# FFN squares, normalised rows and softmax products moved from VectorE to GpSimd in a two-layer attention + FFN kernel

One core of one Trainium2 chip. The metric is the device time of one execution in microseconds (us); lower is better. Every timed run quoted here is of the fast state except where it is said; a program on one core that was run once has no known state.

## What the kernel computes

Two identical layers over x of shape 1 x 2048 x 448 in bf16, each of them attention with 16 heads of 28 and an FFN of 1792:

```python
x = x + A(layernorm(x), wqkv, wo)            # softmax(q k^T * 28**-0.5) v, then wo
x = x + B(layernorm(x), w1, b1, w2, b2)      # relu(x w1 + b1)**2 w2 + b2
# ... the same two lines again
```

Of the kernel before, what the change touches and what calls it, by code (L numbers as in the profile page):

```python
# [13 lines left out]
ALU = mybir.AluOpType  # L14
# [187 lines left out]
def kernel(  # L202
# [12 lines left out]
    nc = tc.nc  # L215
    _, S, D = A_x.shape
# [39 lines left out]
    x_sb = const.tile([P, NTB, D], DT.bfloat16, name="x_sb")  # L256
# [163 lines left out]
    def layernorm(t0, nt, deps_of, early=False, mv=None):  # L420


        if mv is None:
            mv = moments()
            for j in range(nt):
                yield stats(mv, t0, j, deps_of(j))
        ln = {}
        single = early and t0 == 0 and TILES
        rss = []
        for a, b in [(0, 1), (1, 2)] if single else [(0, nt)]:  # L430
            def rsqrt(e, a=a, b=b):
                rstd = sp.tile([P, 4], DT.float32, name="rstd")
                for j in range(a, b):
                    ln[j] = rstd[:, j:j + 1]
                ve = sp.tile([P, 4], DT.float32, name="ve")
                nc.gpsimd.tensor_tensor(out=ve[:, a:b], in0=mv[0][:, a:b, 1], in1=eps_t[:, a:b], op=ALU.add)  # L436
                nc.gpsimd.tensor_tensor(out=rstd[:, a:b], in0=ve[:, a:b], in1=mhalf[:, a:b], op=ALU.pow)  # L437
            rs = Op("POOL", 0.95 if early else 0.6, rsqrt, deps=[mv[1][b - 1]], sets=[("rs", t0 + a)] if early else ())
            rss += [rs] * (b - a)
            pl.spawn(EV, iter([rs]))  # L440
        box = {}

        def take(e):
            box["x"] = xtp.tile([P, NDC, QR], DT.bfloat16, name="xnT")
        own_xt = Op("DVE", 0.0, take, acq=R_xt)
        yield own_xt
        xnT = box["x"]
        ends = []
        todo = []
        evs = []  # L450

        def turn(p0, own, xs):
            box = {}

            def tr(e, xs=xs):
                tp = bank(t, "tp").bitcast(DT.bfloat16).rearrange("p (c q) -> p c q", c=NDC)
                box["t"] = tp
                for k, (xn, _) in enumerate(xs):
                    for dc in range(NDC):
                        nc.tensor.transpose(out=tp[:, dc, k * P:(k + 1) * P],  # L460
                                            in_=xn[:, dc * P:(dc + 1) * P], identity=ident[:, :])
            t = Op("PE", 0.07 * NDC * len(xs), tr, deps=[x[1] for x in xs],
                   acq=pools_now(early) if early else spare(1))
            yield t

            def ev(e, p0=p0, w=len(xs) * P):
                tp = box["t"]
                dst = xnT[:, :, p0 * P:p0 * P + w]
                if e == "ACT":
                    nc.scalar.copy(out=dst, in_=tp[:, :, 0:w])  # L470
                else:
                    nc.vector.tensor_copy(out=dst, in_=tp[:, :, 0:w])
            o = Op("DVE", 0.12 + 0.3 * len(xs), ev, deps=[t], rel=t, sets=[("xT", t0 + p0)] if early else ())
            ends.append(o)
            evs.extend([o, Op("DVE", 0.0, None, deps=[t], rel=own)])

        wide = 1 if single else 2
        for p0 in range(0, nt, wide):
            js = range(p0, min(p0 + wide, nt))
            own = Op("DVE", 0.0, None, acq=R_xn)  # L480
            yield own
            xs = []
            for j in js:
                xn = xns[2 * (own.turn % 2) + j % 2]

                def norm(e, j=j, xn=xn):
                    nc.vector.tensor_scalar(out=xn[:, 0:D], in0=x_sb[:, t0 + j, :],  # L487
                                            scalar1=mv[0][:, j, 0:1], scalar2=ln[j],
                                            op0=ALU.subtract, op1=ALU.mult)
                nm = Op("DVE", 0.42, norm, deps=[rss[j]], sets=[("n", t0, j)] if early else ())  # L490
                yield nm
                xs.append((xn, nm))

            todo.append((p0, own, xs))
            if early and p0 + wide < nt:
                continue
            while todo:
                p0, own, xs = todo.pop(0)
                yield from turn(p0, own, xs)
        yield from evs  # L500
        return xnT, own_xt, ends
# [140 lines left out]
    for pi, (l, qb, g, kbs, first, last) in enumerate(passes):  # L642
        r = 4 // blocks[l][qb][1]
# [182 lines left out]
    oTn_of = {}  # L826
# [81 lines left out]
    def norm_stream(l, qb, g, res, oe):  # L908


        t0, nt = blocks[l][qb]
        n = nt * P
        box = {}
        tail = qb == len(blocks[l]) - 1
        if (l, qb) not in oTn_of:
            def take(e):
                oTn_of[l, qb][0] = np_.tile([P, G, QR], DT.bfloat16, name="oTn")
            oTn_of[l, qb] = [None, Op("DVE", 0.0, take, acq=R_on)]
            yield oTn_of[l, qb][1]
        if tail:  # L920
            def den(e):
                box["t"] = bank(d, "den")
                nc.tensor.matmul(box["t"][:, 0:n], lhsT=sel[:, :], rhs=res["t"][:, 0:n], start=True, stop=True)
            d = Op("PE", 0.1 + n * 4 / 2400, den, deps=[oe], acq=pools_now())
            yield d

            def rcp(e):
                box["r"] = rp.tile([P, QR], DT.float32, name="rec")
                nc.vector.reciprocal(out=box["r"][:, 0:n], in_=box["t"][:, 0:n])  # L929
            r = Op("DVE", n * 0.0066, rcp, deps=[d], rel=d, acq=R_rec)  # L930
            own = r
            yield r
        else:
            w = n // DHP

            def spread(e):
                box["d"] = sp.tile([P, QR // DHP], DT.float32, name="dn")
                nc.sync.dma_start(out=box["d"][:, 0:w],
                                  in_=res["t"][DH::DHP, 0:n])
            d1 = Op("DMA", 0.5, spread, deps=[oe], lat=0.5)  # L940
            yield d1

            def rcp(e):
                nc.vector.reciprocal(out=box["d"][:, 0:w], in_=box["d"][:, 0:w])
            r1 = Op("DVE", 0.25, rcp, deps=[d1])
            yield r1

            def away(e):
                box["s"] = dp.tile([P, w], DT.float32, name=f"scr{w}")
                nc.sync.dma_start(out=box["s"][:, :], in_=box["d"][:, 0:w])  # L950
            d2 = Op("DMA", 0.4, away, deps=[r1], lat=-0.5)
            yield d2

            def back(e):
                box["r"] = rp.tile([P, QR], DT.float32, name="rec")
                src = box["s"][:, :].rearrange("(h a) j -> h (a j)", h=G)
                nc.sync.dma_start(out=box["r"][:, 0:n], in_=src.unsqueeze(1).to_broadcast([G, DHP, n]))
            r = own = Op("DMA", 0.5, back, deps=[d2], acq=R_rec, lat=2.7)
            yield r
        def mul(e):  # L960
            nc.vector.tensor_tensor(out=oTn_of[l, qb][0][:, g, 0:n], in0=res["t"][:, 0:n],  # L961
                                    in1=box["r"][:, 0:n], op=ALU.mult)
        m = Op("DVE", 0.1 + n / 960, mul, deps=[r, oTn_of[l, qb][1]], rel=oe)
        yield m
        yield Op("DVE", 0.0, None, deps=[m], rel=own)
        norm_done.setdefault((l, qb), []).append(m)
        if len(norm_done[l, qb]) == G:
            pl.spawn(LASTP if (l, qb) == (1, len(blocks[1]) - 1) else NLP + 0.1 * (qb - len(blocks[1])) if l == 1 and qb >= len(blocks[1]) - NL else 4 + 0.1 * qb, chain(l, qb))
# [6 lines left out]
    def chain(l, qb):  # L975


        t0, nt = blocks[l][qb]
        n = nt * P
# [20 lines left out]
        for f0 in range(0, NFC, pack):  # L1000
            fcs = range(f0, min(f0 + pack, NFC))
            w = len(fcs) * n
            b = {}
# [7 lines left out]
            def square(e, b=b, w=w, f0=f0):  # L1011
                r = b["r"]
                b["h"] = h = hidden(f0 // pack)
                nc.vector.tensor_tensor(out=h[:, 0:w], in0=r[:, 0:w], in1=r[:, 0:w], op=ALU.mult)

            def then(o, b=b, square=square):
                b["s"] = Op("DVE", 0.42, square, deps=[o], rel=o)
                return b["s"]
            o = yield from mm_tile(
                [(i * n, n, [(w1[:, dc, fc * P:(fc + 1) * P], xnT[:, dc, 0:n]) for dc in range(NDC)])  # L1020
                 for i, fc in enumerate(fcs)],
                relu, 0.70, [*ends, ("w1",)], True, post=[then], acq=R_r)
# [86 lines left out]
```

## The kernel before

All of x, K, Q, V and the weights live in SBUF. The softmax takes no maximum; the row sums come out of the product with V through a column of ones. The order of the instructions on every engine is fixed when the program is built: a planner (a greedy list scheduler) simulates the engines with durations written in the code, and emits instructions in the order in which its simulation starts them. `Op("DVE", 0.42, fn)` means: on VectorE, planned at 0.42 us, emitted by `fn`. Each engine is given its own queue in that order, and semaphores make it wait for what it needs, so a wrong duration does not make a wrong result; it makes an engine stand before something that the plan took for ready.

The parts that matter (cut):

```python
def e_stream():        # ScalarE: exp of three score tiles (128 x 512 each) at a time
    nc.scalar.activation(out=pt[:, 0:n], in_=gbuf[gi]["sc"][:, 0:n], func=AF.Exp, ...)

def a_first / a_rest:  # an "aside": exp of a fourth tile by VectorE, seven instructions
    tensor_scalar(vi<-PSUM); tensor_scalar(vm<-vi); tensor_scalar(vi<-vi)
    3 x scalar_tensor_tensor(vh <- (vh + b) * vm); scalar_tensor_tensor(p <- (vh + b0) * vi)
# an aside is planned only while VectorE's planned load over 12 us is under BUSY=0.95 (or BB=0.85)

def layernorm(...):    # two row tiles j of a block
    norm: nc.vector.tensor_scalar(out=xn[:, 0:D], in0=x_sb[:, t0 + j, :], scalar1=mean, scalar2=rstd,
                                  op0=ALU.subtract, op1=ALU.mult)        # Op("DVE", 0.42)
    tr:   8 x nc.tensor.transpose(out=tp[...], in_=xn[...], identity=ident)  # PE, waits for both norms
    ev:   nc.vector.tensor_copy(out=xnT, in_=tp)                         # then q, k, v or the FFN

def mul(e):            # 1/rowsum, per head group
    nc.vector.tensor_tensor(out=oTn, in0=oT_sb, in1=rec, op=ALU.mult)    # Op("DVE", 0.1 + n / 960)

def square(e):         # FFN
    nc.vector.tensor_tensor(out=h[:, 0:w], in0=r[:, 0:w], in1=r[:, 0:w], op=ALU.mult)  # Op("DVE", 0.42)

def heat():            # extra matmuls on an xn tile, put where the plan has PE idle
```

The softmax here doesn't subtract the row's maximum and nothing guards it: scores larger than these inputs give would overflow.

## Time and profile before

| | before |
|---|---|
| time, median of 2 (range) | 924.38 us (923.94 to 924.81) |
| span of the profiled execution | 921.5 us |
| exponentials on ScalarE | 659 instructions, 886.2 us |
| ScalarE idle just before them | 5.5 us |
| first exponential starts / last one ends before the end of the span | 11.2 us / 17.0 us |
| asides on VectorE | 73 |
| mean granted clock of PE | 1.000 |

How to read it: the last rows make a sum. Head (11.2) + exponentials (886.2) + idle before them (5.5) + tail (17.0) + 1.6 of other ScalarE work between is the span. The same sum for the changed kernel says where its time goes. The tail is found in ScalarE's timeline: twelve exponentials start at 888.94 and last 15.56 us, so the last ends at 904.50. In a line of the waits, the numbers are us in total, times, and the longest:

```profile
ACT pt L755 <- PE sc L737: 3.2, 6, 0.9
```

### The profile page before, as it was taken

How to read it: one execution, taken by the hardware profiler on the slowest of the kernel's cores; microseconds unless marked ns; L12 is line 12 of the kernel's file. 1: busy time of each engine (PE TensorE's matmuls, PEld its weight loads, DVE VectorE, ACT ScalarE, POOL GpSimd, SP SyncE). 2: the span in 40 equal slices, each digit the busy share in tenths (PEclk: the TensorE clock that was granted, in tenths of full speed). 3: DMA queues.
4: the chain of work that ended last, by engine and by line, in shares of the span. 5: the costliest groups of instructions: out<-in, count | busy, mean ns of one | idle time of the engine just before them, and what ended most of it. 6: DMA issues, size and time to landing. Idle time of an engine off the chain costs nothing.

```text
span 921.5 us, 32836 instructions
## 1 busy us (share of the span) xinstructions
PE 860.8 (93%) x14796; PEld 515.4 (56%) x14796; DVE 672.2 (73%) x1387; ACT 896.2 (97%) x678; POOL 39.7 (4%) x89
## 2 busy tenths in 40 slices
PE   8999989999999999899999999989999999999998
PEld 4555656555555555555546455556465465546566
DVE  7754678788877887777857564577887788888355
ACT  6999999999999999999999999999999999999994
POOL 5100000000000000000000000000000000000000
DMA  7200010000000000000000000011000000000100
GB/s 228 64 2 2 3 43 17 15 10 12 15 14 8 14 13 10 14 12 5 2 2 2 2 2 2 6 36 38 16 18 18 28 10 24 14 20 13 25 14 17
DMA packets 33000, 18.67 MB, mean 20 GB/s; under 512 B 17498, under 2 KB 32411, under 8 KB 32860
## 3 DMA queue, kind: packets, MB, share of 16 engines
q1 hardware_dynamic: 32860, 16.58, 6.3%
q8 instruction: 115, 1.88, 0.8%
q14 instruction: 25, 0.20, 0.1%
HBM read 14.26 MB, written 2.07 MB: 18 GB/s over the span
## 4 chain that ended last, share of the span: by engine, by line
ACT 66%; PE 17%; issue 12%; DVE 2%; DMA 2%; POOL 0%; SPq 0%; ACTq 0%; DVEq 0%
ACT pt L755 66%; PE sc L737 6%; PE mt L521 5%; PE oT L878 3%; DMA dn<-oT_sb 2%; PE sc L521 1%; PE tp L460 1%; DVE xn L487 0%; DMA x_sb<-in_A_x_dram 0%; DVE st L414 0%; PE mt L737 0%; DVE oTn L961 0%; PE mt L1060 0%; DVE x_sb L972 0%; POOL rstd L437 0%
## 5 line engine op out<-in xcount | busy, mean ns | idle before, releaser
L755 ACT ACTIVATE pt<-sc 128x1536 bf16<-128x1536 f32 x659 | 886.2, 1508 | 5.5 <-PE sc L737 3.2
L737 PE MATMUL sc<-Q_sb,K_sb 32*128 32x256 bf16 (+1 forms) x7576 | 384.0, 266 | 51.8 <-ACT pt L755 48.7
L737 PEld LDWEIGHTS <-K_sb 32*128 32x128 bf16 x7882 | 214.9, 92 | 218.0 <-issue 209.1
L878 PE MATMUL oT<-pt,V_sb 128*32 128x256 bf16 (+1 forms) x4204 | 149.6, 268 | 0.7 <-DVE rec L929 0.3
L878 PEld LDWEIGHTS <-V_sb 128*32 128x32 bf16 x4352 | 92.5, 96 | 43.6 <-issue 40.9
L521 PE MATMUL mt<-xnT,w 128*128 128x256 bf16 (+1 forms) x896 | 115.7, 270 | 0.6 <-DVE r L1010 0.3
L807 DVE SCALAR_TENSOR_TENSOR vh<-vh,vm 128x512 f32<-128x512 f32 x146 | 99.9, 684 | 1.7
L521 PEld LDWEIGHTS <-w 128*128 128x128 bf16 x952 | 79.4, 98 | 32.0 <-issue 23.3
L1010 DVE TENSOR_SCALAR r<-mt 128x512 bf16<-128x512 f32 x106 | 72.5, 684 | 29.8 <-PE mt L521 29.2
L784 DVE TENSOR_SCALAR vi<-mt 128x512 int32<-128x512 f32 x73 | 50.2, 687 | 31.4 <-PE mt L737 30.0
L972 DVE TENSOR_TENSOR x_sb<-x_sb,mt 128x448 bf16<-128x448 bf16 (+1 forms) x63 | 38.4, 609 | 32.1 <-PE mt L521 31.3
L521 PE MATMUL mt<-w,h 128*128 128x448 bf16 x224 | 52.8, 355 | 0.0
L521 PE MATMUL mt<-w,V_sb 128*128 128x448 bf16 (+1 forms) x224 | 50.8, 351 | 0.0
L807 DVE SCALAR_TENSOR_TENSOR vh<-vm 128x512 f32<-128x512 f32 x73 | 49.6, 680 | 0.0
L737 PE MATMUL mt<-Q_sb,K_sb 32*128 32x256 bf16 (+1 forms) x306 | 48.8, 269 | 0.0
L436 POOL TENSOR_TENSOR ve<-mv,eps_t 128x2 f32<-128x2 f32 (+1 forms) x34 | 8.0, 235 | 867.6 <-DVE mv L415 867.6
L900 DVE COPY oT_sb<-oT 128x256 f32<-128x256 f32 (+1 forms) x48 | 19.2, 400 | 33.2 <-PE oT L878 32.8
L414 DVE BATCH_NORM_STATS2 st<-x_sb 128x6 f32<-128x448 bf16 x64 | 39.3, 615 | 1.3 <-DMA x_sb<-in_A_x_dram 0.8
L543 DVE CAST K_sb<-mt 128x512 bf16<-128x512 f32 (+1 forms) x30 | 20.4, 680 | 21.4 <-PE mt L521 21.3
L487 DVE TENSOR_SCALAR xn<-x_sb,mv,rstd 128x448 bf16<-128x448 bf16 x64 | 25.9, 420 | 10.9 <-POOL rstd L437 8.3
L521 PE MATMUL mt<-xnT,wq 128*128 128x256 bf16 x248 | 33.5, 274 | 0.0
L521 PE MATMUL mt<-xnT,wk 128*128 128x256 bf16 x240 | 32.6, 274 | 0.5 <-DVE K_sb L900 0.4
(89 smaller groups left out, 649.7 us busy)
## 6 DMA issues: line engine op xcount, KB each, us to landing
rec<-scr SPq DMA_DIRECT2D x56, 128.0 KB
x_sb<-in_A_x_dram SPq DMA_DIRECT2D x8, 224.0 KB
out_dram<-x_sb SPq DMA_DIRECT2D x15, 112.0 KB
w<-in_B_w_dram SPq DMA_DIRECT2D x1, 1568.0 KB
w<-in_B_w_dram SPq DMA_DIRECT2D x1, 1344.0 KB
dn<-oT_sb SPq DMA_DIRECT2D x56, 4.0 KB
scr<-dn SPq DMA_DIRECT2D x56, 4.0 KB
V_sb<-in_A_wqkv_dram SPq DMA_DIRECT2D x1, 672.0 KB
```

The lines of the kernel that those rows point to most:

```text
L414: nc.vector.bn_stats(out=st[:, :], in_=x_sb[:, t0 + j, :])
L487: nc.vector.tensor_scalar(out=xn[:, 0:D], in0=x_sb[:, t0 + j, :], scalar1=mv[0][:, j, 0:1], scalar2=ln[j], op0=ALU.subtract, op1=ALU.mult)
L521: nc.tensor.matmul(box["t"][:, c0:c0 + n], lhsT=lhsT() if callable(lhsT) else lhsT, rhs=rhs, start=a, stop=b)
L543: nc.vector.tensor_copy(out=dst, in_=src)
L737: nc.tensor.matmul(dst[k][:, i * nt * P:(i + 1) * nt * P], lhsT=K_sb[l][rows, g, (kb + i) * P:(kb + i + 1) * P], rhs=Q_sb[rows, g, t0 * P: ...
L755: nc.scalar.activation(out=pt[:, 0:n], in_=gbuf[gi]["sc"][:, 0:n], func=AF.Exp, scale=float(np.log(2.0)) * 2.0 ** -23)
L784: nc.vector.tensor_scalar(out=box["i"][:, :], in0=src, scalar1=EXP_BIAS, scalar2=0.0, op0=ALU.add, op1=ALU.max)
L807: nc.vector.scalar_tensor_tensor(out=h[:, :], in0=src, scalar=b, in1=m, op0=ALU.add, op1=ALU.mult)
L878: nc.tensor.matmul(box["t"][DHP * hh:DHP * hh + DHP, 0:n], lhsT=V_sb[l][:, kb + i, 4 * g + hh, :], rhs=p[:, c0:c0 + n], start=begin and kb ...
L900: nc.vector.tensor_copy(out=dst, in_=src)
L972: nc.vector.tensor_tensor(out=x_sb[:, tb, lo:hi], in0=x_sb[:, tb, lo:hi], in1=t[:, 0:hi - lo], op=ALU.add)
L1010: nc.vector.tensor_scalar(out=r[:, 0:w], in0=t[:, 0:w], scalar1=0.0, scalar2=None, op0=ALU.max)
```

## The change

Intent: VectorE carries evacuations from PSUM and the asides; GpSimd is 96% idle. Take elementwise work that touches SBUF alone to GpSimd, and let the planner fill the freed VectorE time with asides. The planner is told what GpSimd is thought to take.

```diff
 def norm(e, j=j, xn=xn):
-    nc.vector.tensor_scalar(out=xn[:, 0:D], in0=x_sb[:, t0 + j, :],
+    (nc.vector if early else nc.gpsimd).tensor_scalar(out=xn[:, 0:D], in0=x_sb[:, t0 + j, :],
                             scalar1=mv[0][:, j, 0:1], scalar2=ln[j],
                             op0=ALU.subtract, op1=ALU.mult)
-nm = Op("DVE", 0.42, norm, ...)
+nm = Op("DVE" if early else "POOL", 0.42 if early else 0.7, norm, ...)
 ...
 def mul(e):
-    nc.vector.tensor_tensor(out=oTn_of[l, qb][0][:, g, 0:n], ...)
+    (nc.vector if tail else nc.gpsimd).tensor_tensor(out=oTn_of[l, qb][0][:, g, 0:n], ...)
-m = Op("DVE", 0.1 + n / 960, mul, ...)
+m = Op("DVE" if tail else "POOL", 0.1 + n / (960 if tail else 400), mul, ...)
 ...
-    nc.vector.tensor_tensor(out=h[:, 0:w], in0=r[:, 0:w], in1=r[:, 0:w], op=ALU.mult)
+    nc.gpsimd.tensor_tensor(out=h[:, 0:w], in0=r[:, 0:w], in1=r[:, 0:w], op=ALU.mult)
-    b["s"] = Op("DVE", 0.42, square, deps=[o], rel=o)
+    b["s"] = Op("POOL", 1.2, square, deps=[o], rel=o)
```

More of the change, by code (lines that the diff above doesn't have):

```diff
@@ L486, in norm @@
                 def norm(e, j=j, xn=xn):
-                    nc.vector.tensor_scalar(out=xn[:, 0:D], in0=x_sb[:, t0 + j, :],
+                    (nc.vector if early else nc.gpsimd).tensor_scalar(out=xn[:, 0:D], in0=x_sb[:, t0 + j, :],
                                             scalar1=mv[0][:, j, 0:1], scalar2=ln[j],
                                             op0=ALU.subtract, op1=ALU.mult)
-                nm = Op("DVE", 0.42, norm, deps=[rss[j]], sets=[("n", t0, j)] if early else ())
+                nm = Op("DVE" if early else "POOL", 0.42 if early else 0.7, norm, deps=[rss[j]], sets=[("n", t0, j)] if early else ())
                 yield nm
@@ L960, in mul @@
         def mul(e):
-            nc.vector.tensor_tensor(out=oTn_of[l, qb][0][:, g, 0:n], in0=res["t"][:, 0:n],
+            (nc.vector if tail else nc.gpsimd).tensor_tensor(out=oTn_of[l, qb][0][:, g, 0:n], in0=res["t"][:, 0:n],
                                     in1=box["r"][:, 0:n], op=ALU.mult)
-        m = Op("DVE", 0.1 + n / 960, mul, deps=[r, oTn_of[l, qb][1]], rel=oe)
+        m = Op("DVE" if tail else "POOL", 0.1 + n / (960 if tail else 400), mul, deps=[r, oTn_of[l, qb][1]], rel=oe)
         yield m
```

## The prediction

> **What bounds the kernel now.** I read the page first: busy shares, the chain that ended last, the groups.
>
> ```profile
> PE 860.8 (93%) x14796; PEld 515.4 (56%) x14796; DVE 672.2 (73%) x1387; ACT 896.2 (97%) x678; POOL 39.7 (4%) x89
> ...
> ACT 66%; PE 17%; issue 12%; DVE 2%; DMA 2%; POOL 0%; SPq 0%; ACTq 0%; DVEq 0%
> ...
> L755 ACT ACTIVATE pt<-sc 128x1536 bf16<-128x1536 f32 x659 | 886.2, 1508 | 5.5 <-PE sc L737 3.2
> L784 DVE TENSOR_SCALAR vi<-mt 128x512 int32<-128x512 f32 x73 | 50.2, 687 | 31.4 <-PE mt L737 30.0
> ```
>
> ScalarE does one exponential after another: 659 instructions fill 886 of 921 us and wait 5.5 us in all. So the time is a head (about 10 us before the exponentials start), the exponentials, and a tail. VectorE is not the bound: nothing that only empties it shows directly. But it takes work from ScalarE. The 73 `vi` instructions are units of scores (128x512) whose exponential VectorE computes, seven instructions each; I call one an aside. An exponential instruction holds three units, so an aside saves ScalarE 886.2/659/3 = 0.449 us.
>
> The schedule is made when the program is built, by a list scheduler with durations written in the code. It admits an aside only when VectorE's planned load over the last 12 us is under 0.95 (0.85 in two stretches), when a PSUM bank is free, and when a buffer for the result is free. That decides what freed VectorE time is worth, so next I asked for busy time by stretches of 40 us, and for the waits of PE.
>
> ```profile
> core 0: us, PE busy (x) PEld busy (x) DVE busy (x) ACT busy (x) POOL busy (x), PEclk, DMA share, GB/s
> ...
> 200.00:240.00 40.00, 38.04 (x612) 21.95 (x600) 33.18 (x69) 40.00 (x31) 1.77 (x4) 1.00 0.05 13
> ...
> 560.00:600.00 40.00, 38.64 (x647) 22.56 (x647) 19.83 (x41) 39.54 (x31) 1.06 (x4) 1.00 0.02 6
> ```
>
> ```profile
> PE sc L737 <- ACT pt L755: 48.7, 129, 0.9
> PE tp L460 <- DVE xn L487: 1.3, 2, 1.1
> ```
>
> There are two kinds of stretch. From 120 to 440 us and from 640 to 840 us VectorE is 80 to 82% busy and 58 of the 73 asides start (the same view restricted to `vi`: 22+12+24); there its load limits them. From 440 to 600 us it falls to 50% with few asides: other gates bind, and freed time buys nothing. PE hardly waits for VectorE, and its whole reserve against ScalarE is 48.7 us.
>
> [...]
>
> ```profile
> L487 DVE TENSOR_SCALAR xn<-x_sb,mv,rstd x64: 365/391/1740, 5.4 to 910.8; 128x448 bf16<-128x448 bf16 x64
> ```
>
> ```profile
> 305.50 0.55 POOL L436 TENSOR_TENSOR ve<-mv,eps_t 128x2 f32<-128x2 f32 x1 [43.26 <-DVE mv L415]
> ```
>
> ```profile
> 305.34 0.66 DVE L807 SCALAR_TENSOR_TENSOR vh<-vm 128x512 f32<-128x512 f32 x1
> ```
>
> The 1740 ns normalisation (median 391; the columns are min/median/max) is one of a run begun at 13.42 us, beside GpSimd's 1.60 us memset of 14.26 us. The 0.55 us GpSimd add (0.20 elsewhere) began inside a two-input VectorE instruction and ended when it did. [...]
>
> **Part by part.** Removed from VectorE: 111 squares of 512 at 0.417 and two of 256 at 0.283 = 46.9 us; 60 normalisations (64 less four marked early) at the median 0.391 = 23.5; 56 products at 0.414 and four narrow ones at 0.280 = 24.3 (the last block of each layer keeps its products). Together 94.7 us in 233 instructions. Neighbours overlap on VectorE by about 0.08 us (starts of 0.42 us instructions are 0.34 apart in the timeline), so the real gain is 94.7 - 233 x 0.08 = 76 us.
>
> Added to GpSimd, [...] product 0.75; normalisation 0.7. Sum 113 x 1.3 + 60 x 0.7 + 60 x 0.75 = 234 us, with the 40 of before 30% of the span. GpSimd is no bound. The diff plans 1.2, 0.7 and 0.74, nearly the same, so the plan is honest about GpSimd [...].
>
> Gain: the same view restricted to the squares puts 36 + 30 = 66 of 113 (58%) in the dense stretches; I take the same share for the rest, so 0.58 x 94.7 = 55 us are freed there. An aside costs 0.687+0.421+0.424+0.680+3 x 0.684 = 4.26 us; 55/4.26 = 13 more if every microsecond were used. Banks and result buffers remain, so I choose 60%: 8 more, 81 in all, minus 8 x 0.449 = **3.6 us**.
>
> [...] One aside spans about 4.8 us (170.53 to 175.33 in the timeline), so 58 x 4.8 = 278 of 520 dense us, 53%. There 66 squares and 68 other moved instructions start, 134; 134 x 0.53 = 71 fall into an aside. If each costs VectorE 0.7 us [...], that is 50 us, against 0.58 x 76 = 44 freed. So VectorE is not really freer, and with 8 more asides is fuller than the plan says. [...] I guess that a quarter of the 50 us reaches PE (12 us) and half of that is taken by PE's reserve: **plus 6 us** of ScalarE idle. This is the softest number.
>
> Cost in the tail, where nothing hides: at the end the last block's FFN has squares at 913.94, 914.83 and 915.88 (two), the last done about 916.5. At 1.3, 1.3, 1.3 and 0.75 us in one queue from 914.0 they end near 918.6; the final products run meanwhile, so about 1.8 us show. Before that, the last block's variance (ready at 909.7) queues behind a square of the block before, and its normalisation is 0.3 us longer: about 1.2. Together **plus 3 us**. The boundary between the layers is lengthened too, but ScalarE idles under 2 us there, and the layer-1 work put ahead covers it.
>
> Sum: 924.4 - 3.6 + 6 + 3 = 929.8, so 930 us.
>
> **Rivals.** First, the freed time becomes asides fully [...]: 13 asides save 5.8 us, tail plus 2, stalls 1: 921.6. For it: VectorE runs ahead of plan, by the 0.08 us overlap of each instruction, and idles 19% even in dense stretches. Against: the 1740 ns instruction. Second, VectorE becomes the bound in the dense stretches, since the plan fills it to 95% [...] clustered waits for two banks could give 0.1 us per exponential in 520 us, 386 x 0.1 = 39 us, making 960. Against: PE waited for VectorE under 5 us before. Third, nothing changes in the count of asides because banks, not load, bind: 924.4 + 5 + 3 = 932. Separately, a changed input to a greedy scheduler with many tuned constants shifts everything; its constants were tuned for the old durations, so a shift is likelier up than down.
>
> **Range and chances.** The first rival sets the low end with some room, 916; half of the second sets the high end, 949. Faster by 2% needs under 906: 40 more asides, three times what the freed time allows: 0.02. Slower by 2% is over 943: stalls of 19 us instead of 6, possible: 0.17. Within 2%: 0.81.
>
> **What would show it.** Right: `vi` count 78 to 86 and exponentials 3 or so fewer; POOL about 30% busy; squares near 1.3 us or above; VectorE's SCALAR_TENSOR_TENSOR and `vm`/`vi` means grown (0.684 and 0.42 before) with maxima over 1.2 us; PE waits on DVE up from under 5 us to 10 to 20; ScalarE idle before exponentials up from 5.5 to about 12; last exponential to end of span longer by 3 us. Wrong: unchanged VectorE maxima [...], the `vi` count flat or up by over 15, squares of 2 us or more, or exponential waits over 20 us.

The durations on GpSimd reckoned with here (square 1.3 us, product 0.75, normalisation 0.7) are my estimates; no trace or run showed them then. The 0.7 us that each moved instruction costs VectorE in an aside is an estimate too; what the trace before showed of VectorE and GpSimd beside each other is the 1740 ns normalisation (median 391) and the 0.55 us add (0.20 elsewhere).

## The result and the profile after

973.55 us, median of 2 (969.21 and 977.89), against 924.38: the ratio is 1.0536 (95% interval 1.0423 to 1.065), slower. Ratios here are the mean time of one kernel's fast runs over that of the other's of the same rounds, so they are not quite the ratio of the medians quoted. A second set on another chip gave 972.93 us and 1.0527 (1.0497 to 1.0558). The result is correct.

The page of the changed kernel, the lines that answer to those of before:

```profile
PE 885.4 (91%) x14630; PEld 521.7 (53%) x14630; DVE 681.1 (70%) x1223; ACT 898.8 (92%) x675; POOL 343.0 (35%) x322
...
ACT 37%; PE 30%; DVE 11%; POOL 9%; issue 9%; DMA 3%; SPq 0%; ACTq 0%; DVEq 0%; POOLq 0%
...
L755 ACT ACTIVATE pt<-sc 128x1536 bf16<-128x1536 f32 x655 | 888.2, 1497 | 54.8 <-PE sc L737 49.0
...
L784 DVE TENSOR_SCALAR vi<-mt 128x512 int32<-128x512 f32 x83 | 57.1, 688 | 32.8 <-PE mt L737 29.6
```

There are ten more asides (83) and four fewer exponentials (655), as intended, and VectorE is no fuller than before (70%). But ScalarE stands idle for 54.8 us before exponentials, and it waits for scores from PE. The sum:

| us | before | after |
|---|---|---|
| head | 11.2 | 11.5 |
| exponentials (count) | 886.2 (659) | 888.2 (655) |
| idle before them | 5.5 | 54.8 |
| tail | 17.0 | 19.0 |
| other | 1.6 | 2.6 |
| span | 921.5 | 976.1 |

49.3 of the 54.6 us are the idle. So the question is what held PE. Its waits in the changed kernel:

```profile
PE sc L737 <- ACT pt L755: 42.3, 107, 0.9
PE tp L460 <- POOL xn L487: 23.1, 19, 2.7
PE mt L1060 <- POOL xn L487: 3.8, 2, 2.5
```

`tp L460` are the transposes of a normalised tile and `xn L487` is the normalisation, now on GpSimd; `mt L1060` is an extra matmul that reads the same tile. Before, PE waited for the normalisation 1.6 us (1.3 of it at `tp L460`, a line in the prediction); now 26.9 us on GpSimd's. The normalisation itself, in the view of its line (minimum/median/maximum):

```profile
L487 POOL TENSOR_SCALAR xn<-x_sb,mv,rstd x60: 1853/1864/2617, 16.3 to 963.8; 128x448 bf16<-128x448 bf16 x60
```

It never took less than 1.85 us, and the plan had 0.7. The two of a block come one after the other, about 4 us where the plan had 1.4. One such place, in the timeline (start, duration, engine, what, and idle before it):

```profile
338.03 1.05 PE L737 MATMUL sc<-Q_sb,K_sb 32*128 32x256 bf16 x24 [0.33 <-ACT pt L755]
...
341.17 4.10 POOL L487 TENSOR_SCALAR xn<-x_sb,mv,rstd 128x448 bf16<-128x448 bf16 x2
...
343.27 0.40 PE L460 MATMUL tp<-ident,xn 128*128 128x128 bf16 x4 [0.23 <-POOL xn L487]
...
345.32 0.61 PE L460 MATMUL tp<-ident,xn 128*128 128x128 bf16 x4 [1.65 <-POOL xn L487]
345.87 0.61 PE L737 MATMUL sc<-Q_sb,K_sb 32*128 32x256 bf16 x6
...
346.58 1.45 ACT L755 ACTIVATE pt<-sc 128x1536 bf16<-128x1536 f32 x1 [1.89 <-PE sc L737]
...
347.38 1.89 PE L737 MATMUL sc<-Q_sb,K_sb 32*128 32x256 bf16 x24
...
349.38 1.45 ACT L755 ACTIVATE pt<-sc 128x1536 bf16<-128x1536 f32 x1 [1.34 <-PE sc L737]
```

PE, in order, stands at the transposes of the second tile until 345.3. The scores queued behind them come late, and ScalarE idles 1.89 us. But it idles again three microseconds later, when PE waits for nothing: the same 24 score matmuls that took 1.05 us at 338.03 take 1.89 us at 347.38. The stretches show why; PEclk is the granted clock of PE:

```profile
core 0: us, PE busy (x) PEld busy (x) DVE busy (x) ACT busy (x) POOL busy (x), PEclk, DMA share, GB/s
320.00:340.00 20.00, 17.97 (x314) 11.62 (x314) 18.09 (x31) 19.89 (x16) 7.78 (x7) 1.00 0.06 15
340.00:360.00 20.00, 18.11 (x214) 8.15 (x209) 11.92 (x21) 15.75 (x13) 6.78 (x6) 0.83 0.03 7
```

The clock fell to 0.83 in this stretch: the trace's clock records have it at one half for 6.8 us from 345.2 on. In the whole span the mean clock is 0.967; by estimate, 976.1 x 0.033 = 32 us of PE work are lost so. The two timed runs go the same way: the one of 969.21 us had a mean clock of 0.981, the one of 977.89 us 0.967. The idle of PE around the start of this half clock is 1.65 us. There are eleven such stretches in this profile, 3.4, 6.8 or 10.2 us long, 64.9 us in all. Eight of them start during a wait of PE for the normalisation on GpSimd or within 1.5 us of its end; the longest of these waits is 2.7 us. There are 21 such waits, so not every one has a half clock with it.

VectorE's instructions that take longer beside GpSimd are in the trace too. Two-input instructions of the asides had maxima of 0.694 us and below before, and now:

```profile
L807 DVE SCALAR_TENSOR_TENSOR vh<-vh,vm x166: 636/692/1418, 110.0 to 893.0; 128x512 f32<-128x512 f32 x166
L807 DVE SCALAR_TENSOR_TENSOR vh<-vm x83: 640/684/1531, 109.1 to 890.6; 128x512 f32<-128x512 f32 x83
```

The one-input `vm` instructions rose from at most 0.43 to 1.02 us.

So three theories stood to be told apart. **A**: the normalisation, 1.2 to 1.9 us longer than planned, stops PE, whose clock is then halved. **B**: GpSimd's work slows the asides and VectorE's evacuations. **C**: the new plan is a worse one, whoever executes it.

### The profile page after: what moved, and what is told of

It reads as the page before. It is cut to its first block, busy times and chain, and to the rows that moved or that the text cites. A ratio compares the mean times of both kernels' runs of the same rounds, so it can differ in the third digit from the quotient of the medians.

```text
span 976.1 us, 32788 instructions
## 1 busy us (share of the span) xinstructions
PE 885.4 (91%) x14630; PEld 521.7 (53%) x14630; DVE 681.1 (70%) x1223; ACT 898.8 (92%) x675; POOL 343.0 (35%) x322
## 3 DMA queue, kind: packets, MB, share of 16 engines
q8 instruction: 114, 1.87, 0.8%
## 4 chain that ended last, share of the span: by engine, by line
ACT 37%; PE 30%; DVE 11%; POOL 9%; issue 9%; DMA 3%; SPq 0%; ACTq 0%; DVEq 0%; POOLq 0%
ACT pt L755 37%; PE mt L521 11%; PE sc L737 11%; POOL xn L487 6%; PE oT L878 5%; DVE vh L807 3%; DVE r L1010 2%; DMA dn<-oT_sb 1%; POOL rstd L437 1%; DVE vi L784 1%; PE tp L460 1%; DVE h L812 1%; POOL V_sb L1014 1%; DVE x_sb L972 1%; PE sc L521 1%
## 5 line engine op out<-in xcount | busy, mean ns | idle before, releaser
L755 ACT ACTIVATE pt<-sc 128x1536 bf16<-128x1536 f32 x655 | 888.2, 1497 | 54.8 <-PE sc L737 49.0
L737 PE MATMUL sc<-Q_sb,K_sb 32*128 32x256 bf16 (+1 forms) x7432 | 386.4, 271 | 44.7 <-ACT pt L755 42.3
L878 PE MATMUL oT<-pt,V_sb 128*32 128x256 bf16 (+1 forms) x4186 | 156.0, 274 | 2.1 <-DVE x_sb L972 1.5
L807 DVE SCALAR_TENSOR_TENSOR vh<-vh,vm 128x512 f32<-128x512 f32 x166 | 132.9, 800 | 3.0
L961 POOL TENSOR_TENSOR oTn<-oT_sb,rec 128x256 bf16<-128x256 f32 (+1 forms) x60 | 48.8, 813 | 228.0 <-DMA rec<-scr 208.2
L487 POOL TENSOR_SCALAR xn<-x_sb,mv,rstd 128x448 bf16<-128x448 bf16 x60 | 119.8, 2004 | 14.6 <-issue 8.9
L1014 POOL TENSOR_TENSOR h<-r 128x512 bf16<-128x512 bf16 x56 | 66.3, 1187 | 145.9 <-DVE r L1010 145.9
L1014 POOL TENSOR_TENSOR V_sb<-r 128x512 bf16<-128x512 bf16 (+1 forms) x57 | 68.3, 1207 | 93.2 <-DVE r L1010 84.7
L784 DVE TENSOR_SCALAR vi<-mt 128x512 int32<-128x512 f32 x83 | 57.1, 688 | 32.8 <-PE mt L737 29.6
L807 DVE SCALAR_TENSOR_TENSOR vh<-vm 128x512 f32<-128x512 f32 x83 | 60.3, 727 | 0.0
L737 PE MATMUL mt<-Q_sb,K_sb 32*128 32x256 bf16 x284 | 48.0, 271 | 0.0
L460 PE MATMUL tp<-ident,xn 128*128 128x128 bf16 x252 | 24.1, 234 | 25.0 <-POOL xn L487 23.1
L900 DVE COPY oT_sb<-oT 128x256 f32<-128x256 f32 (+1 forms) x48 | 19.1, 398 | 37.1 <-PE oT L878 36.5
```

Source lines behind the costliest of these rows:

```text
L460: nc.tensor.transpose(out=tp[:, dc, k * P:(k + 1) * P], in_=xn[:, dc * P:(dc + 1) * P], identity=ident[:, :])
L487: (nc.vector if early else nc.gpsimd).tensor_scalar(out=xn[:, 0:D], in0=x_sb[:, t0 + j, :], scalar1=mv[0][:, j, 0:1], scalar2=ln[j], op0=A ...
L737: nc.tensor.matmul(dst[k][:, i * nt * P:(i + 1) * nt * P], lhsT=K_sb[l][rows, g, (kb + i) * P:(kb + i + 1) * P], rhs=Q_sb[rows, g, t0 * P: ...
L784: nc.vector.tensor_scalar(out=box["i"][:, :], in0=src, scalar1=EXP_BIAS, scalar2=0.0, op0=ALU.add, op1=ALU.max)
L807: nc.vector.scalar_tensor_tensor(out=h[:, :], in0=src, scalar=b, in1=m, op0=ALU.add, op1=ALU.mult)
L878: nc.tensor.matmul(box["t"][DHP * hh:DHP * hh + DHP, 0:n], lhsT=V_sb[l][:, kb + i, 4 * g + hh, :], rhs=p[:, c0:c0 + n], start=begin and kb ...
```

## The experiments

Each kernel was compared with the kernel before on the same chip, whose medians there were 923.15 to 923.72 us. All of them gave correct results.

### e1: normalisations back on VectorE

(Diffs are shortened from here on.)

```diff
-(nc.vector if early else nc.gpsimd).tensor_scalar(out=xn...   # Op("DVE" if early else "POOL", 0.42 if early else 0.7
+nc.vector.tensor_scalar(out=xn...                             # Op("DVE", 0.42
```

> The change without its normalisations: squares and products stay on GpSimd, normalisations go back to VectorE. Theory A (the normalisation takes 1.9 to 2.6 us on GpSimd where the plan has 0.7, PE stands before the transposes, its clock is halved, ScalarE idles): nearly all of the 49 us comes back, 922 to 932 us, clock above 0.99, ScalarE idle before exponentials under 15 us, although two-input VectorE instructions still show maxima over 1.2 us. Theory B [...]: about 180 of 300 us of moved GpSimd work remain, so about 60% of the loss remains, near 953 us. Theory C (the new schedule is a worse one): no sharp number, near 960 if the number of asides is the harm.

Measured: 928.96 us (927.13 to 929.72), ratio 1.0053 (1.0034 to 1.0072), clock 0.998, 80 asides. As A has it, not B. Squares and products are still on GpSimd and VectorE is still slower, in the groups by shape (busy, mean ns) and in ScalarE's waits:

```profile
L807 DVE SCALAR_TENSOR_TENSOR vh<-vh,vm 128x512 f32<-128x512 f32 x160 | 123.3, 771 | 2.4
```

```profile
ACT pt L755 <- PE sc L737: 6.7, 12, 1.1
```

A mean of 771 ns against 684 is 14 us of VectorE time in this group alone, and it costs ScalarE little: idle before exponentials is 10.7 us in all, 5.2 more than before.

### e2: only the normalisations on GpSimd

The complement of e1: `square` and `mul` as before.

> Only the normalisations on GpSimd, planned at 0.7 us as in the change; squares and products stay on VectorE. Theory A: 955 to 972 us, PE waits on the normalisation of 20 us or more, clock 0.96 to 0.98. Theory B: 120 of 300 us of GpSimd work, so 40% of the loss, near 944. Theory C: unclear.

Measured: 964.55 us (962.58 to 965.37), ratio 1.0438 (1.0419 to 1.0457), clock 0.978, as A has it. The normalisations alone cost 40.8 us (964.55 - 923.72), squares and products alone 5.2 us (e1), together 46.0 of the 49 us of the whole change, though each of these kernels has a plan of its own. PE's waits:

```profile
PE tp L460 <- POOL xn L487: 23.7, 19, 2.0
PE sc L460 <- POOL xn L487: 1.9, 1, 1.9
```

PE waits for the normalisation 25.6 us, as in the change, with no square or product ahead of it in GpSimd's queue; so it is not the queue that makes it late. ScalarE's idle before exponentials is 36.5 us, and the tail (last exponential at 937.3 of 962.2) is 24.9 us, 8 longer than before.

### e3: the change, with 2.0 us told to the planner

```diff
-nm = Op("DVE" if early else "POOL", 0.42 if early else 0.7, norm, ...)
+nm = Op("DVE" if early else "POOL", 0.42 if early else 2.0, norm, ...)
```

> The change as it is, but the scheduler is told 2.0 us for a normalisation instead of 0.7; every operation stays on the same engine. Theory A, because the plan then gives PE other work in the meantime: PE waits on normalisations fall from 27 us to under 8, clock above 0.99, 922 to 938 us. Theory B: [...] still 960 to 975.

Measured: 943.87 us (941.62 to 944.79), ratio 1.021 (1.0186 to 1.0234; slower clear of noise, but unclear by the 2% verdict), clock 0.990. No operation changed its engine, but the plan is another one (86 asides); 29 of the 49 us came back. The waits are as expected (5.9 us on the normalisation), the time is not: it lies 6 us over the range of A and 16 under that of B.

```profile
PE tp L460 <- POOL xn L487: 3.1, 3, 2.4
PE mt L1060 <- POOL xn L487: 2.8, 2, 1.5
```

```profile
ACT r L1008 <- PE mt L521: 12.1, 2, 11.8
```

The rest sits in two places that A as I wrote it did not have. The last exponential ends at 914.8 of 942.8, a tail of 28.0 us, 11 more than before. In it ScalarE waits 11.8 us for the first FFN tile after the last exponential. The normalisation ahead of that tile takes 1.87 us of these, about 1.5 more than on VectorE. Most of the rest is the plan: here the output projection and the statistics of that block come after the last exponential (918.3 to 922 us), where in the kernel before the normalisation was done (903.6) before the last exponential ended (904.5), and the wait was 1.75 us. And ScalarE idles 18.1 us before exponentials, 12.6 more than before. So an honest plan hides most of the latency, 26.9 us of waits down to 5.9. How much of the 20 us that remain is the latency and how much the new plan is not shown, as this plan was not run on VectorE.

### e4: the plan of the change, executed by VectorE

The planner keeps "POOL" and the durations of the change; the three instructions are emitted on `nc.vector`, at their places in the emission order.

> The plan of the change to the letter (same order of instructions on every engine, 83 asides), but the moved instructions are executed by VectorE, in the order in which the plan has them. Theories A and B: the loss comes from GpSimd's execution, so it goes: 918 to 932 us, clock above 0.99. Theory C: the loss is in the plan, so 955 to 975 remains.

Measured: 924.81 us (923.63 to 926.3), ratio 1.0012 (0.9992 to 1.0032). C falls for this plan: it costs nothing when the work behind it is fast. Here the plan is held fixed and only the executing engine changes, so the 49 us come from GpSimd's execution. Also, VectorE carried all 83 asides and everything else in that time, busy 77%, and without the moved work on GpSimd the maxima are 0.695 us and below, against 0.694 before:

```profile
L807 DVE SCALAR_TENSOR_TENSOR vh<-vh,vm x166: 640/686/694, 110.4 to 845.4; 128x512 f32<-128x512 f32 x166
L784 DVE TENSOR_SCALAR vi<-mt x83: 655/691/695, 107.9 to 840.9; 128x512 int32<-128x512 f32 x83
```

So the ten asides were gained without need of GpSimd, and gained nothing: exponentials fell from 886.2 to 883.0 us, and idle before them rose from 5.5 to 10.2.

### e5 and e9: PE kept busy in place of waiting

To tell the wait from the halved clock, matmuls without use were put ahead of the transposes; they need nothing from GpSimd, and the transposes overwrite their result. In e5 nine of them (1.7 us) before each of 31 groups of transposes:

```diff
+for _ in range(9):
+    nc.tensor.matmul(tp_bank[:, 0:D], lhsT=ident, rhs=wk[:, 0, 0:14, :], start=True, stop=True)
 for k, (xn, _) in enumerate(xs):   # transposes
```

> The change plus nine matmuls of 448 columns without use (about 1.7 us) on PE ahead of each group of transposes of a normalised block, so that PE works where it stood waiting for GpSimd; the results are overwritten by the transposes. Separates the wait itself from the halved clock that followed it (about 61 us at half clock between 150 and 926 us of the profile of the change). If the halving adds to the loss: time at half clock under 15 us, ScalarE idle before exponentials from 55 to 30 to 40 us, 950 to 962 us. If the wait alone does it: 968 to 985 us, since the useless matmuls also cost time where nothing was waited for.

Measured: 983.55 us (982.1 to 989.05), ratio 1.0662 (1.063 to 1.0695), clock 0.997. The clock came back and the time did not; the number lies in the range of "the wait alone". It still does not decide the question: 31 x 1.7 = 53 us of useless work is about as much as the waits and the halving took together (27 + 32). So e9 put them only where the trace of the change shows a wait, and as many as fill it (12 groups, 116 matmuls, 22 us), with the changed kernel run beside it on the same chip:

> The changed kernel again, so that the next run is compared with it on the same chip: 965 to 980 us.

> The change plus useless matmuls on PE only ahead of those twelve groups of transposes before which the trace of the change shows PE waiting for a normalisation, and only as many as fill that wait (116 matmuls of 0.187 us, 22 us, in place of about 23 us of waits). PE then loses as much time as before to the wait, but does not go idle. If the halved clock is a cost of its own (61 us at half clock are about 31 us of PE work): half-clock time under 15 us, 20 to 32 us faster than the changed kernel on the same chip, near 945. If the waits alone make the loss: within 5 us of the changed kernel.

Measured: the changed kernel 972.93 us (968.44 to 974.47), e9 958.17 us (955.51 to 960.65), ratios 1.0527 and 1.0376 (1.0344 to 1.0407). Of the two profiled runs (`--cores`, and PE's waits for the normalisation), the changed kernel first:

```profile
core 0: 966.7 us, clock 0.977
PE tp L460 <- POOL xn L487: 21.9, 18, 2.7
```

```profile
core 0: 956.2 us, clock 0.991
PE mt L1067 <- POOL xn L494: 3.8, 2, 2.5
PE tp L467 <- POOL xn L494: 0.7, 3, 0.3
```

The edit did what it was for: PE's waits at the transposes are gone, and as much useless work stands in their place. By estimate the clock took 22 us of 966.7 in the one and 9 us of 956.2 in the other. So 13 us less halving go with 10.5 us less time in the profiled pair, and with 14.8 us in the medians: the halving is a cost of its own, a quarter to a third of the loss on this chip. The expectation of 20 to 32 us was too high; this profile of the changed kernel had less half-clock time than the first, on which I had worked it out, and by its mean clock e9 still has 956.2 x 0.009 x 2 = 17 us at half clock, where under 15 were expected.

### e6 and e7: products alone, squares alone

Each is the change with the other two parts put back.

> Only the products with the reciprocal sums on GpSimd (60 instructions near 0.75 us). Theory A: nothing on the path, 922 to 926 us, one to four more asides. Theory B: a few two-input maxima over 1 us and at most 2 us lost.

> Only the squares on GpSimd (113 instructions of 1.04 us[...]). Theory A: 924 to 928 us, a tail about 1 to 2 us longer. Theory B: most of the 5 us that squares and products cost together (0.5%) is theirs, so 926 to 929, with two-input VectorE means near 0.75 us.

Measured: products alone 930.18 us (929.8 to 932.04), ratio 1.0071 (1.0052 to 1.009); squares alone 926.16 us (924.74 to 929.19), ratio 1.0026 (1.0016 to 1.0036). The squares' time lies in the ranges of A and of B and decides nothing. The products are a miss of theory A and not explained by B: the products alone cost more (0.71%) than products and squares together (0.53%), though the moved instructions are 60 and took a median of 0.73 us. In the profile, ScalarE's idle before exponentials is 8.8 us, and the last exponential ends 21.7 us before the end, 4.7 more than before. In the squares' kernel that tail is 19.0 us. Each of these kernels has another plan, and plans alone differ by as much: the tail is 16.9 us in e4 and 24.5 in e10, neither with moved work on GpSimd. So the 0.3 and 0.7% can't be put down to the operations.

### e8: what GpSimd takes for the forms, alone

The kernel before, with 21 GpSimd instructions at its end, where no other compute engine works any more (one run, longer on purpose, state unknown).

> The kernel before with 21 GpSimd instructions added at its end, when nothing else runs, three of each form: the normalisation as it is (two scalars per partition, 448 bf16); on half the width; with one scalar and one operation; with two constants; on fp32; a product of two tensors of 448; a product with one scalar spread by a zero stride. If the cost is per element, the half width takes about 1.0 us, against 1.86; if it is fixed for reading two scalars, about 1.6. If the scalars read per partition cost it, the form with constants takes under 1 us; if it is the pair of operations, the form with one operation does. The span grows by 20 to 35 us on purpose.

The timeline (start, duration of three together):

```profile
918.80 5.79 POOL L1087 TENSOR_SCALAR xn<-x_sb,mbs 128x448 bf16<-128x448 bf16 x3 [7.78 <-issue]
924.69 3.55 POOL L1089 TENSOR_SCALAR xn<-x_sb,mbs 128x224 bf16<-128x224 bf16 x3
928.34 4.41 POOL L1091 TENSOR_SCALAR xn<-x_sb,mbs 128x448 bf16<-128x448 bf16 x3
932.83 5.31 POOL L1093 TENSOR_SCALAR xn<-x_sb 128x448 bf16<-128x448 bf16 x3
938.14 5.78 POOL L1095 TENSOR_SCALAR vh<-vh,mbs 128x448 f32<-128x448 f32 x3
943.89 2.96 POOL L1097 TENSOR_TENSOR xn<-x_sb 128x448 bf16<-128x448 bf16 x3
946.92 2.96 POOL L1099 TENSOR_TENSOR xn<-x_sb,mbs 128x448 bf16<-128x448 bf16 x3
```

From start to start, divided by three: the normalisation as it is (two scalars per partition, two operations) 1.96 us; half the width 1.22; one operation with one scalar 1.50; two constants 1.77; fp32 1.92; a product of two tensors 1.01; the last, a product with one spread scalar, 0.99 by its duration. So it is slow with no other compute engine at work. From the two widths, an estimate: (1.96 - 1.22)/224 = 3.3 ns per element, with 0.48 us fixed. Neither expectation that named one culprit holds: constants instead of scalars save 0.2 us, one operation with one scalar instead of two with two 0.5. A one-input `tensor_scalar` costs up to twice a two-input `tensor_tensor` here (1.96 against 1.01 us).

### e10: more asides by raising the limits

```diff
-BUSY = 0.95   # and BB = 0.85
+BUSY = 1.05   # and BB = 0.95
```

> The kernel before with only the scheduler's two limits for VectorE's planned load raised by 0.10 (0.95 to 1.05, 0.85 to 0.95), GpSimd as before. The run with the plan of the change on VectorE took 924.8 us with 83 asides and VectorE 77% busy, so VectorE has room. If asides are what counts: about 11 more, 5 us less, 917 to 921 us, which would beat both kernels. If the waits and the tail of a fuller plan give it back, as in that run: 922 to 927 us.

Measured: 941.8 us (941.54 to 942.96), ratio 1.0201 (1.0184 to 1.0218), with 82 asides and 656 exponentials: slower clear of noise (unclear by the 2% verdict), and outside both ranges. The loss is no steady one; it is a hole and a tail. ScalarE waits once for 13.6 us near the boundary of the layers, and the last exponential ends 24.4 us before the end (7 more than before):

```profile
560.00:600.00 40.00, 35.29 (x465) 20.42 (x464) 22.85 (x45) 26.44 (x21) 1.06 (x4) 0.96 0.01 2
```

```profile
ACT pt L755 <- PE sc L737: 16.4, 6, 13.6
```

Which rule of the planner makes the hole was not looked into. No version tried beats the kernel before.

## Why the prediction was wrong

The forecast was 930 us (916 to 949); it is 973.55. By its steps:

- **More asides, fewer exponentials: right.** 8 more expected, 10 came (83), with 655 exponentials. The 3.6 us don't appear in the busy time (888.2 against 886.2): count times mean fell by 13.3 us, but the exponentials overlap each other by 92.3 us where it was 107.6. In the working, the squares in the dense stretches are 36 + 34 = 70, not 66 (the stretch from 800 to 840 us was left out); with 70, 59 us would be freed in place of 55, which changes little.
- **Squares and products on GpSimd: about right.** 1.3 us estimated for a square, 1.03 at least for those of 512 into `h` and about 1.2 in the mean (1.19 and 1.23) in the changed kernel; 0.75 for a product, a median of 0.73 and a mean of 0.84 for the wide ones.
- **Normalisation 0.7 us: the step that failed.** It was my estimate, and nothing in the trace before could check it: all 64 normalisations ran on VectorE there, and GpSimd's arithmetic between two tensors was 128 x 2 at the widest. On GpSimd it takes 1.96 us alone (e8) and 1.85 to 2.6 in the kernel. The sentence "so the plan is honest about GpSimd" rested on it. With 2.0 us in the plan, 29 of the 49 us come back (e3); with the normalisations on VectorE, all but 5 (e1).
- **ScalarE idle plus 6 us: wrong, plus 49.** I had derived it from VectorE slowed beside GpSimd, through its late evacuations; that this would reach PE was my guess. PE waited for GpSimd directly: 26.9 us, 23.1 of them at the transposes. That half of the waits would be taken by PE's reserve was wrong as well: PE's waits for scores to be consumed fell only from 48.7 to 42.3 us. The prediction had no term for the clock, which was 1.000 before and 0.967 after; e9 puts it at 10 to 15 us on its chip.
- **PE's waits for VectorE, 10 to 20 us: right by luck.** Summed over the lines of the waits they rose from about 5 to about 15 us. But in e4, where nothing moved to GpSimd and the asides' maxima are those of before, they are about 12 us, and the time is that of before. So most of the rise is the plan's, not GpSimd's, and it cost nothing there.
- **VectorE slower beside GpSimd: right in kind and size, small in effect.** 50 us of VectorE time were expected. Summing count times rise of the mean over the six instructions of an aside that grew gives 19.3 + 3.9 + 5.2 + 3.1 + 11.3 = 43 us (two groups of L807, `vm`, `vi`, and the closing L812); the seventh, `vi<-mt`, took 688 ns against 687. In e1, where part of it remains, the whole loss is 5 us.
- **Tail plus 3 us: right in size** (17.0 to 19.0, and 16.9 in e4 with the same plan on VectorE), though e2 and e3 show that it can be 25 or 28 with another plan.
- **The second rival** had the size (960) and the wrong carrier: VectorE was not the bound at 70%. That its 960 lies nearest is luck. The first rival took 13 more asides for 5.8 us; e4 has ten without freeing any VectorE time, and its time is that of before. Of the prediction's own signs of being wrong, one came: exponential waits over 20 us.

What stays open: the 0.3 to 0.7% of e1, e6 and e7, between slower VectorE instructions and plan, and the exact share of the clock, as the runs of the changed kernel differ in it. Also, e10 lost 18.7 us by its plan alone. So the split of the 49 us between normalisations and the rest, which e1 and e2 read from kernels with plans of their own, is not exact: nobody ran the change's plan with only the normalisations, or all but them, on GpSimd. That the normalisations are the main part rests on PE's waits and on both of these experiments together.

## What to carry to other kernels

In a schedule fixed at build time, a wrong duration costs where an engine stands directly behind the operation: here a factor of 2.7 in one duration made 29 of the 49 us (e3). Ask of each moved operation who waits for it next, not only which engine it frees. Measure the form (operations, scalars, width) on the engine that is to run it before planning with it, as two operations that look alike can differ by two (1.96 against 1.01 us in e8). Idles of PE of at most 2.7 us cost more than their length here, as half clock came with some of them (eight stretches in the changed kernel's profile); filling them with useless matmuls made the kernel 10 to 15 us faster (e9).
